# One group of small matmuls for several: kv of six batches, and the second batch's q, in a fused attention and feed-forward kernel

## The chip, the cores and the metric

The kernel runs on one core of a Trainium2 chip. A core has five engines that run side by side and meet through semaphores: TensorE (PE in the profile; its weight loads are PEld), VectorE (DVE), ScalarE (ACT), GpSimd (POOL) and SyncE (SP, which here only issues DMAs). TensorE writes to PSUM, a small accumulator memory, and DVE or ACT copy results from there to SBUF. The metric is the device time of the kernel in microseconds (us); lower is better.

## The reference

A linear attention without softmax, on 8 batches of 8 heads, 576 rows and 64 columns a head, and behind it a feed-forward block with a SwiGLU over all 4608 rows:

```python
kv = np.einsum('bhsd,bhse->bhde', k, v)          # 64 x 64 for each head
out = np.einsum('bhsd,bhde->bhse', q, kv)
rms = np.sqrt(np.mean(out * out, axis=-1, keepdims=True) + 1e-06)
attn = out / rms * g_norm                        # the heads side by side: x, 4608 x 512

rms = np.sqrt(np.mean(x * x, axis=-1, keepdims=True) + 1e-06)
xn = x / rms * rms_g
g = xn @ w_gate                                  # 512 x 1536
silu = g * (1.0 / (1.0 + np.exp(-g)))
out = (silu * (xn @ w_val)) @ w_out              # 1536 x 512
```

Inputs and output are float32; the kernel's matmuls take bfloat16 and sum in float32.

## The kernel before

The 576 rows of a batch are cut into four chunks of 128 (`NC = 4`) and a remainder of 64. The feed-forward block runs on groups of 512 rows: one group per batch with its four chunks, and a ninth group with the eight remainders. For a group, twelve times a "gate" matmul of four steps and a "val" matmul of four steps (`mm1`, L634) go into one of three `mm1` tiles of PSUM; ACT makes the silu of the gate (L643) and DVE multiplies it with val (L652), which frees the tiles. Then come 48 matmuls with `w_out` (L669, L698), and the rows are copied and stored. The first batch's rows are done in two halves of 256 columns.

The attention of each later batch is laid between the feed-forward matmuls of the batch ahead. A planner does this at build time. The feed-forward work is a list of slots (a gate, a val, a part of the output matmuls; for half of the first batch a gate and a val together). `Placer` gives each slot the attention operations that are emitted with it: those of other engines ahead of the slot's own work, those of TensorE behind it. `P.put` looks for the first slot with room by a table of costs; `P.psum` does so for a TensorE operation that takes one of the three `att` tiles of PSUM; `P.at` puts an operation at a fixed slot. Every engine then runs its list in order. SP and POOL issue the loads, in the order of their own lists.

These are the steps around the change, for one batch:

- `kv_mm` (L268) makes the 64 x 64 product of each head, from k and v that POOL's DMAs have loaded and cast. A head takes five matmuls, one per chunk (the remainder is the fifth), with a result 64 columns wide; the even heads write the lower 64 partitions of the `att` tile and the odd ones the upper. Eight heads make 40 matmuls.
- `kv_half` (L292), two copies on DVE, brings the products to `kvs`.
- q is needed with its columns on the partitions. For the third to eighth batch this is done by DMA (`qT_dma`, L324 and L326). For the second batch it is done on TensorE by `qT_heads` (L309): a matmul with the identity for every head and chunk, again with results of 64 partitions, 40 in all, and copies by DVE and ACT (`qT_out`, L320).
- `o_mm` (L331) multiplies a chunk of q with `kvs`, four matmuls per chunk into one `att` tile. ACT squares it (L357) and copies it (L361); POOL and DVE make the row statistics, DVE scales the rows (L483), and DMAs turn them into the `x` that the next group's gates read. The second batch also has `oT_mm` (L368), which makes the same products turned for its statistics.

`place_attention` lays out the third to eighth batch. It asks for kv in two TensorE operations of cost 0.57, heads 0 to 3 and heads 4 to 7, in one `att` tile; the copies follow the second. `place_second` lays out the second batch at fixed slots. There q's turning is five TensorE operations of eight matmuls in five successive slots, one per pair of heads for the four full chunks and one for the remainder, each with its own `att` tile and one copy, by DVE and ACT in turn. The second batch's kv is one operation of 40 matmuls.

Of the kernel before, what the change touches and what calls it, by code (L numbers as in the profile page):

```python
# [86 lines left out]
def kernel(  # L87
# [17 lines left out]
    NC = 4  # L105
    MAIN = 128 * NC
    REM = S - MAIN
    NS = d_model // 128
# [433 lines left out]
    def place_casts(P, b, at=0):  # L542
        if b == 2:
            for n, hs in enumerate((H0, H1)):
                P.at("ACT", 1.04, lambda hs=hs: cast_main(b, 0, nc.scalar, hs), at + n)
            op = P.at("ACT", 0.62, lambda: cast_rem(b, 0, nc.scalar), at + 2)
            return [op, ("DMA", at + 11)]
        ops = [P.put("POOL", 1.1, lambda hs=hs: cast_main(b, 0, nc.gpsimd, hs), at=at) for hs in (H0, H1)]
        return [P.put("POOL", 0.65, lambda: cast_rem(b, 0, nc.gpsimd), at=ops[1][1])]
# [3 lines left out]
    def place_attention(P, b, casts=(), at=0, chain_at=0):  # L553
        a = Att(b)
        V, A = nc.vector, nc.scalar
        N1 = range(NC + 1)
        P.floor = max(P.floor, at)
        load = P.put("SP", 0.0, a.qT_dma, casts[:1] if b == 2 else casts)
        qt = [("DMA", load[1] + QT_SLOTS)]
        p0 = P.psum(0.57, lambda: a.kv_mm((0, 1)), casts)  # L560
        p1 = P.reads(P.put("PE", 0.57, lambda: a.kv_mm((2, 3)), [p0], at=p0[1]))
        kv = [P.reads(P.put("DVE", 0.4, lambda h=h: a.kv_half(h), [p1])) for h in range(2)]
        outs, reds = {}, []
        for c in N1:
            p = P.psum(0.24, lambda c=c: a.o_mm(c), kv + qt)
            s = P.reads(P.put("ACT", 0.6, lambda c=c: a.sq_(c), [p]))
            outs[c] = P.reads(P.put("ACT", 0.6, lambda c=c: a.outa_(c), [p]))
            w = P.put("POOL", 1.2, lambda c=c: a.wsq(c, nc.gpsimd), [s])
            reds.append(P.put("DVE", 0.68, lambda c=c: a.red(c, 0), [s]))
            reds.append(P.put("DVE", 0.68, lambda c=c: a.red(c, 1), [w]))  # L570
        prev = reds
        for n in range(0, 13, 4):
            prev = [P.put("DVE", 0.8, lambda n=n: [f() for f in a.chain(0, NC + 1)[n : n + 4]], prev, chain_at)]
        xn = [P.put("DVE", 0.68, lambda c=c: a.xna_(c, V), prev + [outs[c]]) for c in N1]
        put = [P.put("SP", 0.0, lambda c=c: a.x_dma(*c), [xn[c[1] - 1]]) for c in ((0, 2), (2, 4), (4, 5))]
        return put[1][1] + X_SLOTS

    def place_second(P, s):
        a = Att(1)
        V, A = nc.vector, nc.scalar  # L580
        engs = {"DVE": V, "ACT": A}
        ps = {}
        pe = lambda at, cost, n, fn: P.at("PE", cost, lambda: ps.__setitem__(n, fn()), s + at)
        dve = lambda at, cost, fn: P.at("DVE", cost, fn, s + at)
        act = lambda at, cost, fn: P.at("ACT", cost, fn, s + at)

        for j in range(NS):
            pe(j - 5, 0.25, ("q", j), lambda j=j: a.qT_heads((j,), range(NC)))
            if j % 2:
                act(j - 4, 0.58, lambda j=j: a.qT_out(ps["q", j], (j,), 0, A))  # L590
            else:
                dve(j - 4, 0.42, lambda j=j: a.qT_out(ps["q", j], (j,), 0, V))
        pe(-1, 0.25, ("q", NC), lambda: a.qT_heads(ALL, (NC,)))
        act(0, 0.58, lambda: a.qT_out(ps["q", NC], ALL, NC, A))
        P.at("PE", 1.14, lambda: a.kv_mm(range(NS)), s + 2)
        dve(3, 0.43, lambda: a.kv_half(0))
        dve(3, 0.43, lambda: a.kv_half(1))

        parts = [((j,), 0, NC) for j in range(NS)] + [(ALL, NC, NC + 1)]
        oT = lambda n: pe((3, 4, 4, 5, 6)[n], 0.25, ("oT", n), lambda: a.oT_mm(*parts[n]))  # L600
        o = lambda n: P.at("PE", 0.24, lambda: a.o_mm(n), s + (3, 4, 5, 5, 6)[n])
        for f, n in ((oT, 0), (o, 0), (oT, 1), (o, 1), (oT, 2), (o, 2), (oT, 3), (o, 3), (oT, 4), (o, 4)):
            f(n)
        for n in range(NC + 1):
            act((4, 5, 5, 6, 7)[n], 0.62, lambda n=n: a.sqT_(ps["oT", n], *parts[n]))
            dve((4, 5, 6, 6, 7)[n], 0.69, lambda n=n: a.outa_(n, V))
        P.at("PE", 0.64, lambda: a.stat_mm(0, NC + 1, True), s + 8)
        act(8, 1.28, lambda: A.preload_act_table(ACT.Sqrt))
        dve(9, 2.0, lambda: a.lead_chain(0, NC + 1))
        for c in range(NC + 1):  # L610
            dve(10 + c, 0.68, lambda c=c: a.xna_(c, V))
        for at, cs in ((15, (0, 1)), (17, (2, 3))):
            for js, eng in ((P0, "ACT"), (P1, "DVE")):
                P.at("PE", 0.24, lambda js=js, cs=cs: a.xT_mm(js, cs), s + at)
                for j in js:
                    P.at(eng, 0.4, lambda j=j, cs=cs, e=engs[eng]: a.xT_out(j, cs, e), s + at + 1)
        P.at("PE", 0.15, lambda: a.xT_mm(ALL, (NC,)), s + 19)
        dve(20, 0.62, lambda: [a.xT_out(j, (NC,), V) for j in ALL])
        P.floor = s + 20
        return s + 18  # L620
# [136 lines left out]
    V, G, A = nc.vector, nc.gpsimd, nc.scalar  # L757
    H0, H1 = (0, 4), (4, 8)
    P0, P1 = (0, 1), (2, 3)
    ALL = range(NS)  # L760
# [30 lines left out]
    a = Att(0)  # L791
# [52 lines left out]
    for n, w in enumerate(FB):  # L844
        js = range(FB0[n], FB0[n] + w)
# [66 lines left out]
    P = Placer(slots, 3)  # L912
    casts = ()
    for b in range(1, B):
        if b == 1:
            end = place_second(P, 9)
        else:
            s0 = starts[b - 1]
            end = place_attention(P, b, casts, s0 - 2, s0 + 2 * NF - 4)
        if os.environ.get("PLACER"):  # L920
            print("batch", b, "to", end, "wanted at", starts[b], "casts", casts)
        else:
            assert end < starts[b] + (b == 1), (b, end, starts)
        if b == 1:
            for n, at in ((0, 6), (1, 24), (2, 30), (3, 40)):
                for j in range(NS):
                    for w, eng, cost in ((wg, "DVE", 0.09), (wv, "ACT", 0.13)):
                        f = P.put(eng, cost * FB[n], lambda w=w, n=n, j=j, e=eng: fold(w[n], j, e), at=starts[1] + at + j)
                        assert f[1] < starts[2] + (2 * FB0[n] if n == 3 else 0), f
            casts = place_casts(P, 2, starts[1] - 9)  # L930
        elif b + 1 < B:
            P.put("SP", 0.0, lambda b=b: load_q(b + 1), at=starts[b - 1] + 6 * (b == 2))
            casts = place_casts(P, b + 1, starts[b - 1] + 18)
            for f in loads_kv(b + 1):
                P.put("POOL", 0.85, f, at=starts[b - 1] + 14)
# [29 lines left out]
```

## Time and profile before

Three runs took 329.0, 329.57 and 476.69 us; the median is 329.57.

| | us |
|---|---|
| profiled execution | 329.4 |
| its span, first to last instruction | 327.6 |
| PE busy | 318.6 |
| DVE busy | 176.0 |
| ACT busy | 144.5 |
| POOL busy | 89.0 |
| kv products (L268), 280 | 7.6 |
| q's transposes on TensorE (L309), 40 | 5 groups of 0.41 |

The span is counted from the first instruction on any engine to the end of the last. Matmuls overlap in their pipeline: a matmul of 512 columns is shown with 379 ns, while its successor starts 216 ns after it. So busy time says little of the pace, and the distance between the starts of two matmuls is what to read. The granted TensorE clock is 0.998 of full speed over the span.

### The profile page before, as it was taken

How to read it: one execution, taken by the hardware profiler on the slowest of the kernel's cores; microseconds unless marked ns; L12 is line 12 of the kernel's file. 1: busy time of each engine (PE TensorE's matmuls, PEld its weight loads, DVE VectorE, ACT ScalarE, POOL GpSimd, SP SyncE). 2: the span in 40 equal slices, each digit the busy share in tenths (PEclk: the TensorE clock that was granted, in tenths of full speed). 3: DMA queues.
4: the chain of work that ended last, by engine and by line, in shares of the span. 5: the costliest groups of instructions: out<-in, count | busy, mean ns of one | idle time of the engine just before them, and what ended most of it. 6: DMA issues, size and time to landing. Idle time of an engine off the chain costs nothing.

```text
span 327.6 us, 5425 instructions
## 1 busy us (share of the span) xinstructions
PE 318.6 (97%) x2060; PEld 162.2 (49%) x2060; DVE 176.0 (54%) x392; ACT 144.5 (44%) x269; POOL 89.0 (27%) x109
## 2 busy tenths in 40 slices
PE   7789999999999999999999999999999999999995
PEld 2468765554445444544454445444544444444443
DVE  3458446679928681768077807781687234203411
ACT  1375446776658422842274227421752233223320
POOL 8663320028205800580058004900420000000000
PEclk9999999999999999999999999999999999999999
DMA  8999999774994895589557966696000800020013
GB/s 193 227 200 199 194 223 212 179 175 53 167 208 136 103 157 161 145 98 140 161 167 84 136 166 176 70 148 168 35 1 0 170 32 0 13 116 2 0 34 96
DMA packets 78741, 40.49 MB, mean 124 GB/s; under 512 B 42744, under 2 KB 74236, under 8 KB 78716
## 3 DMA queue, kind: packets, MB, share of 16 engines
q0 software_dynamic: 30928, 14.16, 34.2%
q1 hardware_dynamic: 46048, 25.08, 31.9%
q10 hardware_dynamic: 1740, 0.92, 1.0%
q8 instruction: 16, 0.26, 0.3%
q14 instruction: 9, 0.07, 0.1%
HBM read 37.78 MB, written 9.44 MB: 144 GB/s over the span
## 4 chain that ended last, share of the span: by engine, by line
PE 94%; DMA 3%; DVE 1%; issue 0%; POOL 0%; ACT 0%; DVEq 0%; POOLq 0%
PE mm L634 57%; PE o L669 26%; DMA vc<-in_v_dram 3%; PE att L331 2%; PE att L268 2%; PE mm L669 2%; PE o L698 1%; PE att L309 1%; PE o L368 0%; DVE xna L350 0%; PE att L509 0%; PE mm L279 0%; PE att L368 0%; PE mm L662 0%; PE mm L232 0%
## 5 line engine op out<-in xcount | busy, mean ns | idle before, releaser
L652 DVE TENSOR_TENSOR h<-silu,mm 128x512 bf16<-128x512 bf16 (+1 forms) x120 | 75.7, 632 | 79.6 <-PE mm L634 69.3
L643 ACT ACTIVATE silu<-mm 128x512 bf16<-128x512 f32 (+1 forms) x120 | 66.4, 556 | 89.1 <-PE mm L634 80.2
L634 PE MATMUL mm<-x,wv 128*128 128x512 bf16 (+1 forms) x432 | 99.8, 355 | 0.0
L634 PE MATMUL mm<-x,wg 128*128 128x512 bf16 (+1 forms) x420 | 98.7, 358 | 0.0
L669 PE MATMUL o<-wo,h 128*128 128x512 bf16 x396 | 89.9, 379 | 0.0
L414 POOL TENSOR_TENSOR sq<-sq,g 128x512 bf16<-128x512 bf16 x30 | 34.4, 1153 | 134.2 <-ACT sq L357 134.2
L634 PEld LDWEIGHTS <-wg 128*128 128x128 bf16 x468 | 45.0, 98 | 45.9
L634 PEld LDWEIGHTS <-wv 128*128 128x128 bf16 x480 | 45.4, 98 | 40.9
L669 PEld LDWEIGHTS <-h 128*128 128x128 bf16 x420 | 40.3, 98 | 46.9
L685 ACT COPY osb<-o 128x512 f32<-128x512 f32 x33 | 19.3, 589 | 67.8 <-PE o L669 67.8
L419 DVE TENSOR_REDUCE st<-sq 128x8 f32<-128x512 bf16 x60 | 38.4, 679 | 0.0
L292 DVE CAST kvs<-att 64x256 bf16<-64x256 f32 x14 | 5.9, 422 | 39.5 <-PE att L268 39.4
L483 DVE TENSOR_TENSOR xna<-outa,al 128x512 bf16<-128x512 bf16 x35 | 21.8, 686 | 0.0
L357 ACT ACTIVATE sq<-att 128x512 bf16<-128x512 f32 x30 | 18.2, 607 | 0.0
L361 ACT CAST outa<-att 128x512 bf16<-128x512 f32 x30 | 17.8, 594 | 0.0
L331 PEld LDWEIGHTS <-qTs 128*128 128x128 bf16 x140 | 9.8, 98 | 5.2
L634 PE MATMUL mm<-xr,wg 128*128 128x512 bf16 x48 | 12.3, 379 | 0.0
L634 PE MATMUL mm<-xr,wv 128*128 128x512 bf16 x48 | 12.3, 379 | 0.0
L331 PE MATMUL att<-kvs,qTs 128*128 128x128 bf16 x140 | 11.7, 219 | 0.0
L203 POOL CAST main_q<-stg 128x1024 bf16<-128x1024 f32 (+1 forms) x12 | 11.4, 987 | 0.1
L232 PE MATMUL mm<-idle 128*128 128x512 bf16 x27 | 8.0, 455 | 2.1 <-DVE idle L161 2.1
L786 ACT ACTIVATE wv<-wv,gain 128x384 bf16<-128x384 bf16 x16 | 9.2, 612 | 0.2 <-PE mm L634 0.2
(130 smaller groups left out, 175.4 us busy)
## 6 DMA issues: line engine op xcount, KB each, us to landing
out_dram<-osb SPq DMA_DIRECT2D x32, 256.0 KB, 2.3
stg<-in_q_dram SPq DMA_DIRECT2D x6, 1024.0 KB, 6.8
vc<-in_v_dram POOLq DMA_DIRECT2D x7, 512.0 KB, 8.4
kc<-in_k_dram POOLq DMA_DIRECT2D x7, 512.0 KB, 6.2
wg<-in_moe_w_gate_dram POOLq DMA_DIRECT2D x4, 384.0 KB, 16.1
wv<-in_moe_w_val_dram POOLq DMA_DIRECT2D x4, 384.0 KB, 17.1
wo<-in_moe_w_out_dram POOLq DMA_DIRECT2D x4, 384.0 KB, 13.6
stg<-in_k_dram SPq DMA_DIRECT2D x2, 512.0 KB, 7.1
```

Of the source, the lines that this page charges most:

```text
L203: return copy(out=mains[b, t][:, cs[0] : cs[1], h0:h1, :], in_=staged[b, t].rearrange("p h (c d) -> p c h d", c=NC)[:, cs[0] : cs[1], h0:h ...
L331: nc.tensor.matmul(o[:, 2 * j : 2 * j + 2, :], lhsT=self.qTj[:, j, c, :], rhs=self.kv[:, j, :, :], start=j == 0, stop=j == NS - 1, skip_gr ...
L357: nc.scalar.activation(out=self.sq[c][:, 0], in_=self.o[c], func=ACT.Square)
L361: (eng.tensor_copy if eng else nc.scalar.copy)(out=self.outa[c], in_=self.o[c])
L414: eng.tensor_tensor(out=self.sq[c][:, 1], in0=self.sq[c][:, 0], in1=g2, op=OP.mult)
L419: nc.vector.reduce_sum(out=self.st[:, which, c, :], in_=self.sq[c][:, which], axis=AX.X)
L483: return eng.tensor_tensor(out=self.xna[:, c], in0=src, in1=self.al[:, c, :].to_broadcast([128, H, D]), op=OP.mult)
L634: nc.tensor.matmul(ps[:, : c1 - c0], lhsT=w[n][:, s, jj * 128 : (jj + 1) * 128], rhs=x_of(g, s, c0, c1), start=s == 0, stop=s == NS - 1)
L643: nc.scalar.activation(out=sis[g, j][:, c0:c1], in_=ps, func=ACT.Silu)
L652: nc.vector.tensor_tensor(out=hs[g, j][:, c0:c1], in0=sis[g, j][:, c0:c1], in1=v_ps, op=OP.mult)
L669: nc.tensor.matmul(ps, lhsT=hs[g, j][:, t * 128 : (t + 1) * 128], rhs=wo[j // OB][:, j % OB, :], start=j == 0, stop=j == NF - 1)
L685: (eng.copy if eng is nc.scalar else eng.tensor_copy)(out=o, in_=ps)
```

## The change

Two things are joined. In `place_attention` the planner is asked for one TensorE operation of all eight heads, of cost 1.2, in place of two of 0.57; the two copies depend on it. In `place_second` the five turning operations become one, `turn_q`, at a fixed slot, one slot behind that of the first of the five before. It takes three `att` tiles: two pairs of heads with their four chunks in each of the first two, and all heads' remainder in the third. DVE copies the first tile in two operations and ACT the second, in the two slots that follow; ACT copies the third in the slot behind those. The number and the shapes of matmuls and copies stay.

```diff
         qt = [("DMA", load[1] + QT_SLOTS)]
-        p0 = P.psum(0.57, lambda: a.kv_mm((0, 1)), casts)
-        p1 = P.reads(P.put("PE", 0.57, lambda: a.kv_mm((2, 3)), [p0], at=p0[1]))
-        kv = [P.reads(P.put("DVE", 0.4, lambda h=h: a.kv_half(h), [p1])) for h in range(2)]
+        p = P.psum(1.2, lambda: a.kv_mm(ALL), casts)
+        kv = [P.reads(P.put("DVE", 0.4, lambda h=h: a.kv_half(h), [p])) for h in range(2)]
...
-        for j in range(NS):
-            pe(j - 5, 0.25, ("q", j), lambda j=j: a.qT_heads((j,), range(NC)))
-            if j % 2:
-                act(j - 4, 0.58, lambda j=j: a.qT_out(ps["q", j], (j,), 0, A))
-            else:
-                dve(j - 4, 0.42, lambda j=j: a.qT_out(ps["q", j], (j,), 0, V))
-        pe(-1, 0.25, ("q", NC), lambda: a.qT_heads(ALL, (NC,)))
-        act(0, 0.58, lambda: a.qT_out(ps["q", NC], ALL, NC, A))
+        def turn_q():
+            for n, (js, chunks) in enumerate(((P0, range(NC)), (P1, range(NC)), (ALL, (NC,)))):
+                ps[n] = a.qT_heads(js, chunks)
+
+        P.at("PE", 1.2, turn_q, s - 4)
+        for j in range(2):
+            dve(-3 + j, 0.42, lambda j=j: a.qT_out(ps[0][:, j : j + 1], (j,), 0, V))
+            act(-3 + j, 0.58, lambda j=j: a.qT_out(ps[1][:, j : j + 1], (2 + j,), 0, A))
+        act(-1, 0.58, lambda: a.qT_out(ps[2], ALL, NC, A))
         P.at("PE", 1.14, lambda: a.kv_mm(range(NS)), s + 2)
```

`P0`, `P1` and `ALL` are the pairs of heads (0, 1), (2, 3) and 0 to 3; `s` is 9. In the order in which the planner puts things, the copies of kv and the first L331 groups of the third to eighth batch also stand one slot earlier than before, and the later L331 groups of the fifth to eighth batch are spread otherwise over the same slots.

## The prediction

> **What bounds the kernel now.** I read the page from its busy times to the chain of work that ended last, then the chain in order of time, then TensorE's timeline around the groups that the change joins.
>
> ```profile
> span 327.6 us, 5425 instructions
> PE 318.6 (97%) x2060; PEld 162.2 (49%) x2060; DVE 176.0 (54%) x392; ACT 144.5 (44%) x269; POOL 89.0 (27%) x109
> PE 94%; DMA 3%; DVE 1%; issue 0%; POOL 0%; ACT 0%; DVEq 0%; POOLq 0%
> ```
>
> TensorE is busy for 97% of the span and is 94% of the chain; the other engines are near half. Busy time alone doesn't say that TensorE is at its peak, so I looked at the starts of its matmuls. From 25 to 323 us they follow each other at the step that their width gives: 216 ns for 512 columns, 109 ns for 256, 56 ns for 128. The exceptions are one wait of 0.44 us at 46.6 us (for the second batch's kv to be copied), the small statistics group near 52.8 us, three transposes near 30 us, and the two ends of every group with 64-wide results: the groups of this change. In the chain in order of time, each line gives start, length and work:
>
> ```profile
> 37.03 0.34 PE att L309 x8
> 37.37 0.98 PE mm L634 x8
> 38.35 0.34 PE att L309 x8
> ...
> 45.40 0.83 PE att L268 x40
> ...
> 64.74 0.49 PE att L268 x20
> 65.23 0.97 PE mm L634 x4
> 66.20 0.49 PE att L268 x20
> 66.69 1.83 PE mm L634 x8
> ```
>
> Here is the whole case. Twenty kv products (L268) take 0.49 us, but forty, in the second batch, take 0.83 us and not 0.98; four wide matmuls ahead of such a group take 0.97 us where undisturbed ones take 0.86 us. So a group has a fixed price at each end. The timeline of TensorE, whose starts I use below (start, length, count), shows it more sharply:
>
> ```profile
> 36.43 0.60 PE L634 MATMUL mm<-x,wv 128*128 128x256 bf16 x4
> 36.96 0.41 PE L309 MATMUL att<-ident,qc 128*64 128x128 bf16 x8
> 37.31 0.61 PE L634 MATMUL mm<-x,wg 128*128 128x256 bf16 x4
> 37.75 0.60 PE L634 MATMUL mm<-x,wv 128*128 128x256 bf16 x4
> 38.28 0.41 PE L309 MATMUL att<-ident,qc 128*64 128x128 bf16 x8
> ```
>
> Four undisturbed 256-column matmuls take 0.44 us from start to start (37.31 to 37.75); with a turning group behind them it is 0.53 (37.75 to 38.28). A step from a 128-wide to a 64-wide shape leaves 0.09 us in which nothing starts, and the step back about 0.10.
>
> **kv of the third to eighth batch.** By the trace's starts in ns, the last wide matmul ahead of a group of 20 stands 802 ns before the first one behind it (64.358 to 65.160; 65.819 to 66.621), where 216 is normal; the first one behind then takes 11 ns too long. A group of 20 so costs 802 - 216 + 11 = 597 ns. The group of 40 in the second batch, between 256-column and 512-column work: 46.135 - 45.123 = 1012, less 109, plus 10: 913 ns. Twice 597 is 1194, so one group of 40 for two of 20 saves 0.281 us. Six batches: **1.69 us**. The number of products is the same; the twenty more cost 316 ns, 15.8 each. The third to eighth batch have the shapes and row counts of the second, so no bound further off than its row is needed: 1.6 to 1.8 us.
>
> A rule speaks against this price. The Trainium skill, "TensorE: Matmul & The Clock Gate", section "Wait — 56ns, not 53.3ns?", has a floor of about 25 ns between the starts of two matmuls however few columns they have. By it twenty more products would cost 0.50 us, a batch would save 0.10 and six 0.6. The trace disagrees: 15.8 ns, with the two halves' products in pairs 26 ns, then 5 ns apart.
>
> **The second batch's q.** Five groups of eight transposes (L309) become one of forty, a slot after the first one's present place. From 36.757 (last wide start) to 37.306 (next) is 549 ns; less 109, plus 11, a group costs 0.451 us and five cost 2.26. In a group a pair of transposes starts 80 ns after the first pair, then 56 and 55 ns after the one before. At 55.5 ns a pair, 32 more transposes cost 0.89 us, the one group 1.34, and **0.92 us** is saved. No row shows forty transposes in a run. Bounds: the first pair's 80 ns throughout (group 1.73, saving 0.52), and the 15.8 ns of a kv product (group 0.96, saving 1.30). I take 55.5 ns, the row of the same instruction in steady state.
>
> **What moves with it.** In the built order of the changed kernel TensorE has the same instructions, q's forty in one run and kv's forty in one run per batch. DMAs and casts keep their order on SP and POOL, and nothing is moved past either queue. Nothing is added, so what can be lost is cover:
> - Data. q's first transposes now start near 37.8 us and the short last chunk's near 38.8 instead of 42.3. Their loads landed at 33.71 and 34.09: 4 us of cover. Everything behind comes 0.9 us earlier against loads paced from outside: k and v of the second batch landed by 40.78 for a need at 45.3, w_out's first quarter at 42.65 for 46.1. All stay hidden. v's last rows for the fourth batch land at 92.18 for 94.0, the smallest margin of a later batch; the loads behind it have 9 to 10 us. Its issue on POOL stands behind multiplies and casts that come earlier too.
> - Buffers of the turn. All three `att` tiles are taken at once; the next to want one is kv, six slots later. ACT now copies in three slots running: a copy spaced 0.54 us and a silu of 0.39 make 0.93 us a slot, against 0.875 of TensorE. From the starts above, ACT trails by some 0.1 us at the third, and the tightest release of an `mm1` buffer (DVE's product of the third slot behind the turn, for the gate two slots on) comes some 0.05 to 0.1 us early, 0.18 in the present rhythm. If that cover goes, 0.1 us a slot is lost, at most 0.4.
> - Buffers of the batches. The kv copies on DVE (0.42 us each) now run a slot earlier, behind the one group, and end some 1.4 us before the first product of q and kv (L331), also placed a slot earlier. q's transposed load for the third batch has moved its last packet at 62.8 us; the need is now about 66.4. Of the five L331 groups the fourth and fifth want buffers that ACT's copies free: about 0.9 and 1.3 us of margin. An L331 group costs nothing at its ends: its steps stay at 56 ns, same 128-wide shape. So nothing for either.
> - Behind 323.8 us (last copy and store) nothing changes.
>
> **The sum.** The profiled execution took 329.4 us, its span 327.6; 1.8 us lie around it and stay. 329.4 - 1.69 - 0.92 = 326.8. The median of the runs shown, 329.57, is 0.17 higher and would give 327.0; I say **326.9**, 0.8% below. With the bounds of the q term (-0.38, +0.40), 0.1 for kv and 0.3 for the spread of undisturbed runs (329.0 to 329.57), its own range is 326.1 to 327.8.
>
> **Rivals.**
> 1. The evacuation of the turn stalls TensorE: ACT's and DVE's copies, packed into three slots, hold `mm1`. For: the margins of under 0.1 us. Against: three buffers, and ACT idle 0.94 us today ahead of each silu without a copy in front. Price 0.4 us, at worst a whole copy, 0.59: 327.3 to 327.5. Chance 0.05.
> 2. The run of transposes slows TensorE's clock. In the first microseconds matmuls of 512 columns stood 402 to 427 ns apart instead of 216, eight times running (2.1 to 5.5 us), though the granted clock reads 1.00. One such spell costs 8 x 0.211 = 1.7 us: 328.6. Against: groups of q, up to 0.35 us long, have no such trace behind them, and the new one is 1.3. Chance 0.03. The same page's section "Part 4: PE-mode transpose" says that transposes don't count as work for the gate, and its Part 1 sets a window of 3.4 us; no run here has a turn that long, and by that the gate should hold too.
> 3. On the other side: slower than before. The fourth batch's v lands too late. Its main load took 8.2 us from issue to landing, later ones 7.8 to 9.95. The one group of 40 needs all heads at once, but so did the first of the two. TensorE would stall by what the landing slips beyond 1.85 us, and the gain is gone from 1.85 + 2.6 = 4.5 us of slip; each further us costs one (6.5 us of slip: 331.4), and past 11 us it is 2% slower. Against: the issue moves with the work that it stands behind, and the largest slip seen is 1.8. Chance 0.02.
> 4. It doesn't give what the groups of 20 suggest: the ends cost as much inside one long group. The second batch's 40 speaks against. For kv nothing would be saved: 328.5. Chance 0.02.
>
> **How the numbers follow.** Forecast 0.88, rivals 0.05, 0.03, 0.02 and 0.02. Range 325.9 to 328.2: forecast and first rival, with a little below. 2% of this kernel, 6.6 us, is about what a measurement of it can tell from no change; all cases lie within it but the far end of the third rival. Faster by over 2% 0.01 (for what no case foresees), within 0.98, slower 0.01.
>
> **What would show it.** In the changed profile's chain: L268 x40 of 0.83 us in all seven batches, one pair of stretched neighbours each; one L309 x40 of about 1.2 us near 37.9; no new wait of TensorE between 39 and 43 us or at L331; TensorE's matmuls the same in number, the span 2.6 us shorter. Wrong would be a step over 56 ns per pair of transposes, gaps ahead of gates after the turn, or a wait for v near 92 us.

## The result, and the profile after

The changed kernel takes 326.64 us (median of four runs, 326.35 to 327.13), against 329.31 us for the kernel before (median of three runs, 329.0 to 329.57): a ratio of 0.9919, with a 95% interval of 0.9907 to 0.9931. A fourth run of the kernel before, a slow one of 476.69 us, is left out of this comparison. The changed kernel is 0.8% faster, which is within 2%.

The changed kernel's page, its span, its busy times and the shares of the chain that ended last by engine:

```profile
span 324.6 us, 5420 instructions
PE 316.2 (97%) x2060; PEld 162.2 (50%) x2060; DVE 177.0 (55%) x392; ACT 144.5 (45%) x269; POOL 89.4 (28%) x109
PE 95%; DMA 3%; DVE 1%; issue 0%; POOL 0%; ACT 0%; DVEq 0%; POOLq 0%
```

The number of matmuls is as before, TensorE is as busy in share, and it has 2.4 us less of busy time. Its chain in order of time (start, length, work) has at the joined places:

```profile
31.81 5.68 PE mm L634 x52
37.49 1.24 PE att L309 x40
38.73 5.35 PE mm L634 x48
44.07 0.83 PE att L268 x40
...
63.41 0.81 PE att L268 x40
64.22 1.83 PE mm L634 x8
66.05 0.22 PE att L331 x4
...
92.42 0.81 PE att L268 x40
93.23 0.75 PE o L669 x3
93.98 1.73 PE mm L634 x8
95.71 0.45 PE att L331 x8
...
125.53 0.81 PE att L268 x40
```

There is one line of forty where there were two of twenty, and one turn of 1.24 us where there were five of 0.34. Behind the turn, 48 wide matmuls take 5.35 us, 0.11 each: no stall there.

The two spans differ by 3.0 us, more than the 2.6 that the change explains. The chain tells the rest from the change. The stretch of wide matmuls behind the last transposes of the first batch starts at 32.23 us before and at 31.81 after. From there to the end it is 327.6 - 32.23 = 295.37 before and 324.6 - 31.81 = 292.79 after, **2.58 us** less. The other 0.42 us lie ahead of the change, where the loads of the first rows and weights set the pace: the chain's wait for the first batch's v is 9.27 us before and 8.82 after.

### The profile page after: what moved, and what is told of

Its sections match the earlier page's. It is cut to its first block, busy times and chain, and to the rows that moved or that the text cites. A ratio compares the mean times of both kernels' runs of the same rounds, so it can differ in the third digit from the quotient of the medians.

```text
span 324.6 us, 5420 instructions
## 1 busy us (share of the span) xinstructions
PE 316.2 (97%) x2060; PEld 162.2 (50%) x2060; DVE 177.0 (55%) x392; ACT 144.5 (45%) x269; POOL 89.4 (28%) x109
## 4 chain that ended last, share of the span: by engine, by line
PE 95%; DMA 3%; DVE 1%; issue 0%; POOL 0%; ACT 0%; DVEq 0%; POOLq 0%
PE mm L634 57%; PE o L669 26%; DMA vc<-in_v_dram 3%; PE att L331 2%; PE att L268 2%; PE mm L669 2%; PE o L698 1%; PE att L509 1%; PE o L368 0%; PE mm L279 0%; PE att L368 0%; PE mm L662 0%; PE att L309 0%; PE mm L232 0%; PE att L340 0%
## 5 line engine op out<-in xcount | busy, mean ns | idle before, releaser
L634 PEld LDWEIGHTS <-wv 128*128 128x128 bf16 x480 | 46.2, 98 | 44.0
L331 PEld LDWEIGHTS <-qTs 128*128 128x128 bf16 x140 | 10.3, 98 | 6.6
L331 PE MATMUL att<-kvs,qTs 128*128 128x128 bf16 x140 | 12.7, 219 | 0.0
## 6 DMA issues: line engine op xcount, KB each, us to landing
wg<-in_moe_w_gate_dram POOLq DMA_DIRECT2D x4, 384.0 KB, 15.8
```

What stands on the lines that cost most here:

```text
L331: nc.tensor.matmul(o[:, 2 * j : 2 * j + 2, :], lhsT=self.qTj[:, j, c, :], rhs=self.kv[:, j, :, :], start=j == 0, stop=j == NS - 1, skip_gr ...
L634: nc.tensor.matmul(ps[:, : c1 - c0], lhsT=w[n][:, s, jj * 128 : (jj + 1) * 128], rhs=x_of(g, s, c0, c1), start=s == 0, stop=s == NS - 1)
```

## The experiments

The theory: a step between matmuls whose results are 128 wide and ones whose results are 64 wide costs about 0.1 us each way, whatever stands in the group. (Width here is the number of partitions that a result takes.) The rivals are that the gain came from something else that moved, that crowded copies give a part of it back, that the price is one of any group, and that long runs of transposes slow the clock.

### One part alone

The first kernel has only the joined kv, the second only the joined turn:

```diff
+        p = P.psum(1.2, lambda: a.kv_mm(ALL), casts)     # first kernel: this, and the turn as before
...
+        P.at("PE", 1.2, turn_q, s - 4)                   # second kernel: this, and kv as before
```

> Only kv is joined (third to eighth batch), q of the second batch is turned in five groups as before. Theory (each group of 64-wide results costs a fixed price at its two ends, and the two parts add): 329.44 - 1.69 = 327.75 us, ratio 0.995, and six switches into 64-wide work fewer than before, none else. Rival (the gain of kv came from the other spread of the q-and-kv products, L331, or from an earlier start of the loads): the number of stretched steps falls as well, but the time does not follow it: outside 327.5 to 328.0.

> Only q of the second batch is turned in one group; kv of the third to eighth batch stays in two groups of 20. Theory: 329.44 - 0.92 = 328.5 us, ratio 0.997. Rival (with three copies in a row on ACT and two on DVE a part of the gain is lost to stalls of the mm1 buffers): 328.7 to 328.9, with gaps ahead of gates behind the turn.

With kv alone it is 327.62 us (327.26 to 327.89), ratio 0.9944 [0.9932, 0.9957]: 1.66 us less than the 329.28 measured beside it, where 1.69 was expected. With the turn alone it is 328.37 us, ratio 0.9968 [0.9957, 0.9980]: 0.91 us less, where 0.92 was expected. The two parts add up to 2.57 us. The chain of the kernel with the turn alone shows it beside kv in the old form:

```profile
37.89 1.24 PE att L309 x40
44.47 0.83 PE att L268 x40
63.81 0.49 PE att L268 x20
65.27 0.49 PE att L268 x20
```

So neither part needs the other, and no part of the turn's gain is given back by ACT's and DVE's copies.

### More groups

The changed kernel, with kv of the third to eighth batch in four groups:

```diff
-        p = P.psum(1.2, lambda: a.kv_mm(ALL), casts)
+        p = P.psum(0.3, lambda: a.kv_mm((0,)), casts)
+        for j in (1, 2, 3):
+            p = P.reads(P.put("PE", 0.3, lambda j=j: a.kv_mm((j,)), [p], at=p[1] + 1))
```

> The changed kernel, but kv of the third to eighth batch in four groups of ten products with feed-forward work between. Theory (fixed price per group, whatever its length): three more groups per batch, 6 x 3 x 0.281 = 5.06 us more than the changed kernel, 331.7 us, and each group of ten about 0.33 us long in the chain. Rival (the price grows with the length of the group, or a wait of the group's first product makes it): less, 326.6 to 329.

It took 337.35 us, ratio 1.0237 [1.0221, 1.0253]: 5.6 us more than the theory's 331.7. The steps at the groups of the later batches are as expected, 93 ns missing ahead of each and 95 behind. The rest sits in one place. First the line of the waits (us in total, times, the longest), then the timeline of TensorE (start, length; in brackets the idle time ahead and what ended it):

```profile
PE att L268 <- DMA vc<-in_v_dram: 3.7, 2, 2.8
```

```profile
83.82 9.44 PE L671 MATMUL o<-wo,h 128*128 128x512 bf16 x43
96.06 0.28 PE L268 MATMUL att<-vc,kc 128*64 128x64 bf16 x4 [2.79 <-DMA vc<-in_v_dram]
97.26 0.48 PE L268 MATMUL att<-vc,kc 128*64 128x64 bf16 x6 [0.92 <-DMA vc<-in_v_dram]
98.07 1.06 PE L671 MATMUL o<-wo,h 128*128 128x512 bf16 x2 [0.33 <-issue]
99.06 0.56 PE L268 MATMUL att<-vc,kc 128*64 128x64 bf16 x10
99.55 1.89 PE L636 MATMUL mm<-x,wg 128*128 128x512 bf16 x4
```

TensorE waits for the fourth batch's v, which landed at 95.92 (its main rows) and 97.22. Four wide matmuls then take 1.89 us by this view instead of 1.03. The windows of that stretch give the busy times of TensorE, its weight loads, DVE, ACT and POOL, and then the granted clock (the column ahead of the last two, which are of the DMAs):

```profile
88.00:93.00 5.00, 5.00 (x25) 2.18 (x23) 2.31 (x8) 2.19 (x4) 0.00 (x0) 1.00 1.41 188
93.00:97.50 4.50, 0.79 (x12) 0.47 (x10) 0.00 (x0) 0.00 (x0) 0.00 (x0) 0.91 1.48 146
97.50:104.00 6.50, 6.17 (x46) 2.42 (x45) 0.19 (x1) 2.70 (x5) 0.00 (x0) 0.54 0.77 230
```

The clock loses 0.09 of 4.5 us and 0.46 of 6.5 us here. At half clock that is 0.8 and 6.0 us: with hardly any work from 93.3 us on, the clock falls to half near 96.7 and comes back near 103.5. The steps between wide matmuls are 400 to 427 ns there, where 216 is normal. That agrees with the Trainium skill, "TensorE: Matmul & The Clock Gate", Part 1: an idle window of about 3.4 us halves the clock.

Why is v late? In the list of POOL the fourth batch's loads stand behind the third batch's multiplies. With four groups the third batch's squares come later, and so do the multiplies: POOL issued k's main rows at 81.09 us where the changed kernel has 75.51, and v's main rows at 82.71 against 80.83. All four loads then ran together, and v's main rows took 13.2 us to land instead of 8.4.

The next kernel takes that away. POOL gets the loads ten slots earlier, ahead of the multiplies; TensorE's order stays:

```diff
-                P.put("POOL", 0.85, f, at=starts[b - 1] + 14)
+                P.put("POOL", 0.85, f, at=starts[b - 1] + (4 if b == 2 else 14))
```

> As the run with kv in four groups of ten, but POOL issues the fourth batch's loads of k and v ten slots earlier, ahead of the third batch's multiplies instead of behind them; TensorE's order is the same. Theory (of the 10.7 us that the four groups cost against the changed kernel, 5.1 are the price of 18 groups, and the rest is a single wait for the fourth batch's v near 93 us with a spell of half clock behind it): 326.64 + 5.06 = 331.7 us, to 332.2 us with the wait for the weights near 28 us, no wait at 93 us, granted clock 1.00 throughout. Rival (the price per group of ten is itself about 0.6 us): 337 us again.

It took 331.91 us (331.58 to 332.08), ratio 1.0079 [1.0064, 1.0094]. The wait is gone, and the windows over the same place stay at full clock:

```profile
94.00:98.00 4.00, 3.84 (x51) 1.95 (x51) 0.29 (x1) 2.70 (x5) 0.00 (x0) 1.00 0.59 183
98.00:104.00 6.00, 6.00 (x41) 3.18 (x40) 4.80 (x10) 4.38 (x9) 2.31 (x2) 1.00 0.58 175
```

Against 326.61 us for the changed kernel measured beside it (below) 18 groups cost 5.30 us, 0.29 each, where 0.28 was the price worked out from groups of 20. The price is one per group. The late load explains the other 5.4 us between the two medians. The profile of the late load is that of its slowest run, 338.18 us, and shows more. From the wide matmuls behind the first batch's last transposes (31.82 us there, 32.47 with the early loads) to the ends of the spans (336.4 and 330.3) the two differ by 6.75 us. Of these 4.0 are the two gaps ahead of v's products (2.95 and 1.09 beyond the normal step), and the remaining 2.7 the slow spell.

### Is it the shape?

In the next two kernels each kv product takes a stationary side of 128 columns and writes all 128 partitions, so that nothing in `kv_mm` is 64 wide; kv is made in two groups of twenty or in one of forty. The stationary side holds the product's own chunk and a neighbour, so the values of kv are not the reference's.

```diff
                 for c in self.kv_chunks:
                     cols = slice(c * D, (c + 1) * D)
+                    two = slice(min(c, NC - 1) * D, min(c, NC - 1) * D + 2 * D)
                     nc.tensor.matmul(
-                        self.kv_ps[rows, h // 2, at], lhsT=k_[:, h, cols], rhs=v_[:, h, cols],
+                        self.kv_ps[:, h // 2, at], lhsT=k_[:, h, two], rhs=v_[:, h, cols],
```

> The changed kernel, but every kv product has a stationary side of 128 columns (its chunk of k and the next one) and writes all 128 partitions, and the third to eighth batch make it in two groups of 20 with feed-forward work between. The numbers computed for kv are not the reference's; the work after it is the same. To be read against the run with one group of 40. Theory (the price is the change of shape between 128-wide and 64-wide results): no stretched step at the ends of any kv group, and the same time as with one group of 40, within 0.3 us. Rival (the price is paid at each change of operands or group, whatever the shape): 6 x 0.28 = 1.7 us more than with one group of 40.

> As the run with two wide groups, but one group of 40 wide kv products in each of the third to eighth batch; the numbers computed for kv are not the reference's. Theory: no stretched step at the ends; the products themselves are slower than the pairs of 64-wide ones, 29 ns by their 64 columns to 56 ns (the step of L331, if the weight load sets the pace), so 40 take 1.2 to 2.2 us instead of 0.91, times seven: 2 to 9 us more than the changed kernel, 328.6 to 335.7 us. Rival: 0.2 us at the ends of each group on top.

Two groups took 328.40 us (ratio 0.9971 [0.9959, 0.9984]) and one group 328.85 us (0.9982 [0.9970, 0.9993]). Two groups are not slower than one. The 0.45 us between them are more than the 0.3 of the theory, but they lie the other way, and the intervals overlap. The traces place them ahead of the groups: from the wide matmuls behind the first batch's last transposes (32.02 and 32.62 us in the two chains) to the last matmul both kernels take the same time, to 0.01 us. The timeline of TensorE with two groups (start, length, shape, count):

```profile
127.67 1.03 PE L636 MATMUL mm<-x,wg 128*128 128x512 bf16 x4
128.53 0.75 PE L269 MATMUL att<-vc,kc 128*128 128x64 bf16 x20
129.11 1.03 PE L636 MATMUL mm<-x,wv 128*128 128x512 bf16 x4
129.97 1.03 PE L636 MATMUL mm<-x,wg 128*128 128x512 bf16 x4
```

From 127.67 to 128.53 are 0.86 us, four undisturbed steps, and from 128.53 to 129.11 are 0.58, twenty steps of 29 ns. Nothing is lost at either end. So the price in the kernel before is the step between the two widths, not the group, its operands or its semaphores. The Trainium skill says this in "TensorEngine Tiling (Array Packing)", section "Key Properties": a change of the tiling mode drains TensorE. It gives no price; here it is 0.09 us on the way in and 0.10 on the way back.

The same two runs show what 64-wide results are worth: forty wide products take 1.17 us, the narrow ones 0.91 with both ends. In two groups of twenty it is 1.17 against 1.19. So for the third to eighth batch narrow products had hardly an advantage in the kernel before; they have it in one group.

### A longer run of transposes

The turn of the second batch four times over, into the same tiles:

```diff
-                ps[n] = a.qT_heads(js, chunks)
+                ps[n] = a.qT_heads(js, chunks, 4)     # each transpose of the tile four times
```

> The changed kernel, but the second batch's q is turned four times over into the same tiles, 160 transposes in one run instead of 40 (the output is the same). Theory: 120 more at 27.9 ns, 3.35 us more, 330.0 us, and the wide matmuls behind the run step at 109 ns from the first. Rival (a run of transposes this long, 4.6 us, does not count as work and the clock of TensorE falls): the transposes in the later part, or the wide matmuls behind, step at about double for some us; 1.7 us or more on top, 331.7 us and over.

It took 330.46 us, ratio 1.0033 [1.0021, 1.0045]: 3.8 us more than the changed kernel. The chain gives the turn with 4.59 us against 1.24, the expected 3.35 to the hundredth:

```profile
32.21 5.68 PE mm L635 x52
37.88 4.59 PE att L310 x160
42.47 5.35 PE mm L635 x48
```

The 48 wide matmuls behind it take 5.35 us, as behind the short turn, and the granted clock of both stretches is 1.00. The remaining 0.47 us are not at the turn. Beside the changed kernel's second profile (below), 0.21 are one longer step at 97.3 us (428 ns in place of 216, ahead of a gate; its cause stays open), and nothing else behind 32 us differs. The wait for weights near 28.5 us (see the last section) is as long in both. The rival of the slow clock falls. The Trainium skill's remark that transposes don't engage the clock gate as work does ("TensorE: Matmul & The Clock Gate", "Part 4: PE-mode transpose") makes no difference here over 4.6 us, in any of five runs (330.29 to 330.60).

### What is left around the turn

Two kernels take the reading further. One makes the second batch's kv a slot earlier, so that its copies are done when they are needed. The other moves the turn to stand right in front of kv, in one run of 80 narrow matmuls; the turned remainder goes to a tile of the pool of the output matmuls, since all three `att` tiles are taken:

```diff
-        P.at("PE", 1.14, lambda: a.kv_mm(range(NS)), s + 2)
+        P.at("PE", 1.14, lambda: a.kv_mm(range(NS)), s + 1)      # first kernel; the copies a slot earlier too
...
-                ps[n] = a.qT_heads(js, chunks)
+                ps[n] = a.qT_heads(js, chunks, o2_p if n == 2 else None)
+            a.kv_mm(range(NS))
-        P.at("PE", 1.2, turn_q, s - 4)
+        P.at("PE", 2.1, turn_q, s - 1)                           # second kernel; kv's copies at s + 1
```

> The changed kernel with the second batch's kv one slot earlier, so that its copies have a slot of feed-forward work in front of the first matmul that needs them. Theory: the one wait of TensorE left behind 25 us (0.44 us, for the copies of kv) goes: 326.64 - 0.44 = 326.2 us. Rival (what follows is late by itself, the squares and copies of the second batch): the wait moves on, 326.6 us.

> The changed kernel with the second batch's turn of q moved four slots later less one, right in front of its kv, which comes three slots earlier, so that both make one run of 80 matmuls with 64-wide results; the turned remainder goes to a tile of the output matmuls' pool. Theory: the wait for the copies of kv goes (0.44 us) and one pair of ends (0.2 us): 326.0 us, one stretched step into 64-wide work where there were two. Rival (seven copies of DVE and ACT in three slots hold the buffers): stalls of 0.3 to 1 us there, 326.3 to 327.

The first took 326.47 us (ratio 0.9907 [0.9892, 0.9922]), the second 326.12 us (0.9897 [0.9882, 0.9911]). In the first the step of 656 ns ahead of the first L368 is gone from the trace, and no other wait stands in its place; but its time is only 0.14 us below the 326.61 of the changed kernel's second measurement (below), where 0.44 was expected, and too little to tell. From 32 us to the last matmul its trace is 0.45 us shorter than that kernel's second one, so that the wait did go and did not move on. The second was run once more beside the changed kernel:

> The changed kernel once more, beside the two others of this call: 326.6 us, 0.8% faster than before.

> The run with the second batch's turn and kv in one run of 80, once more beside the changed kernel. Theory: 0.65 us faster than the changed kernel (the wait of 0.44 us for the copies of kv, and one pair of ends), 326.0 us. Rival (the copies' crowd gives it back): the same as the changed kernel.

The changed kernel took 326.61 us (326.38 to 326.75), ratio 0.9919 [0.9904, 0.9934]; the other 325.82 us (325.79 to 325.83), ratio 0.9895 [0.9879, 0.9912]. Each of its runs is below the lowest of the changed kernel, and the difference of 0.79 us is near the 0.65 expected. The same kernel took 326.12 us in its first measurement, so the runs alone say 0.5 to 0.8; by the traces, from 32 us to the last matmul, it is 0.67. It beats both kernels. Its chain at the place:

```profile
40.22 1.01 PE att L309 x32
41.24 0.22 PE o L309 x8
41.46 0.69 PE att L268 x40
42.15 0.99 PE mm L634 x8
```

Transposes and products stand side by side with no gap between them: both are 64 wide. There is one pair of ends where there were two.

## Why the prediction was right

The forecast was 326.9 us, with 325.9 to 328.2, and 326.64 was measured; a second measurement gave 326.61. The sum itself said 326.8. The 0.17 that moved it to 326.9 came from a median of three runs with the one of 476.69 us among them, and led away from the result.

**The price of the ends.** 1.69 us for six batches; kv alone measured 1.66. The step behind it, that a group costs a fixed price at its two ends, was read from the second batch's one group of 40 beside the others' groups of 20. The four groups with early loads confirm it for groups of ten, and the wide products show that it belongs to the shape.

**The pace of the long turn.** 0.92 us, from 55.5 ns per pair; alone it measured 0.91. In the changed kernel's trace the pairs stand 80 ns, then 55 or 56 ns apart, and the turn costs 1443 - 109 + 10 = 1344 ns, where 1.34 us was worked out. The bounds for an unseen run of forty (0.52 and 1.30) were not needed.

**The cover of the copies.** Here a step was mis-sized, on the safe side. I took ACT's slot at 0.93 us, a copy spaced 0.54 and a silu of 0.39. ACT's timeline in the changed kernel:

```profile
38.55 0.58 ACT L320 COPY qTs<-att 128x512 bf16<-128x512 bf16 x1 [1.07 <-PE att L309]
39.31 0.38 ACT L643 ACTIVATE silu<-mm 128x256 bf16<-128x256 f32 x1 [0.18 <-PE mm L634]
39.59 0.58 ACT L320 COPY qTs<-att 128x512 bf16<-128x512 bf16 x1
40.18 0.38 ACT L643 ACTIVATE silu<-mm 128x256 bf16<-128x256 f32 x1
40.46 0.58 ACT L320 COPY qTs<-att 128x512 bf16<-128x512 bf16 x1
41.05 0.38 ACT L643 ACTIVATE silu<-mm 128x256 bf16<-128x256 f32 x1
```

A silu with work right behind it takes 0.28 us from start to start, not the 0.38 of its record; a copy takes 0.59 until the next silu starts, which comes with TensorE's rhythm (the gate that starts at 39.54 ends at 40.14, and its silu starts at 40.18). In the kernel before a copy took 0.54. The slot is 0.87 us, that of TensorE, and ACT never trails. I had used the distance for the copy and the whole record for the silu.

**The kv of the batches.** No wait of TensorE appears at any L331 group, and none at kv. That the five groups are spread otherwise costs nothing, as worked out.

**The rivals.** The stall of the turn did not come (the turn alone gave 0.91 of 0.92). The slow clock was excluded by the run of 160. Its example was misread, though: the steps of 402 to 427 ns in the first microseconds are not shown to be at full clock. The view prints 1.00 where the trace has no record of the clock, and the first record, of full clock, is at 5.61 us, just where the steps turn to 216 ns. The half clock behind the late v gives the same 400 to 427 ns. That the ends cost as much inside a long group was excluded by kv alone. The late v did not come in the changed kernel, but the run with four groups shows the mechanism. Its margin shrank, which I had not worked out: v's last rows land at 91.14 for a first product at 92.35, 1.2 us, where it was 1.8 before. The loads moved up by 1.0 us and TensorE by 1.6. And its price was sized too low: "each further us costs one" leaves out the clock, which fell to half in a stall of 4.0 us and made it 6.7.

**The sum.** The distance from the profiled execution's own time held to 0.03 us from 32 us to the end (2.58 for 2.61). That the span fell by 3.0 is not part of it. The same comparison, from the first wide matmul behind the last transposes of the first batch to the start of the last matmul, leaves out what the first loads do:

| | expected, us | by the traces, us |
|---|---|---|
| changed kernel against before | -2.61 | -2.60 |
| kv alone against before | -1.69 | -1.68 |
| turn alone against before | -0.92 | -0.91 |
| four groups with early loads against the changed kernel | +5.06 | +5.03 |
| two wide groups against one | 0 | 0.00 |
| turn four times against the changed kernel | +3.35 | +3.56 |

Only the last differs, by the longer step at 97.3 us.

## What to carry to other kernels

Where TensorE is the bound and its matmuls stand at their normal steps, look at the starts around small groups. A pair of lines like x20 in 0.49 and x40 in 0.83 us shows a fixed price at the ends, and it can be saved by putting work of the same output width side by side, even work of different kinds.

When an operation of TensorE is spread or moved, follow the list of the engine that issues the next loads. Spread operations delayed the squares, those POOL's multiplies, and those a load, and that cost as much as all the ends together.

## What was not expected of the hardware

- A narrow product costs 15.8 ns in a stream that uses both halves of the partitions, a wide one with the same 64 moving columns 29.2 ns. The narrow ones start 26 and 5 ns apart in turn, as two series side by side, each with steps of 31 to 32 ns. Taken together, 15.8 ns is below the floor of 25 ns of the Trainium skill ("TensorE: Matmul & The Clock Gate", "Wait — 56ns, not 53.3ns?"), by which the joined kv would have given 0.6 us; it gave 1.66.
- A stall of 4.0 us cost 2.7 us more through the clock, whose granted value was 0.54 over the 6.5 us from 97.5 us on.
- Near 28.5 us, where the last quarters of the gate weights land, TensorE waits 0.37 to 0.61 us in every profile of an experiment, the changed kernel's second one among them (0.49), and in neither of the two profiles of before and after that are compared above. A difference of spans of half a microsecond between two profiles therefore says nothing of a change behind that place; the steps of TensorE and the distance to the end from a common point do.
